# Transposing the gates of a recurrence on two row tiles of TensorE instead of the whole array

## Chip, cores and metric

The kernel runs on one NeuronCore of a Trainium2 chip. The metric is the device time of one execution in microseconds (us); lower is better. The engines are named as in the profile: PE is TensorE (PEld its weight loads), DVE is VectorE, ACT is ScalarE, POOL is GpSimd, SP issues the DMAs.

## What is computed

Two layers stand one after the other, on 4 batches of 6272 time steps and 256 channels, in float32. The first is a gated recurrence over time, the second a long convolution written with Fourier transforms:

```python
sig = 1 / (1 + exp(-f_logit))
f = lower_bound + (1 - lower_bound) * sig
i = 1 - f
for t in range(S):                      # S = 6272
    h = f[:, t] * h + i[:, t] * x[:, t]
    y[:, t] = h
...
proj = y @ w_proj                       # 256 -> 768
x1, x2, x3 = the three thirds of proj
conv = irfft(rfft(x2, axis=1) * rfft(filter, axis=0), n=S, axis=1)
out = (x1 * conv * x3) @ w_out
```

## The kernel before

**An order written by a list scheduler.** The kernel's text does not issue instructions in the order of its loops. Each step is registered with `op(kind, cost, fn, r=, w=, take=, src=)` in a `Plan`: its kind, its assumed cost on each engine that may run it, what it reads and writes, how many of the 8 PSUM banks it takes (`take`), and, for a reader of such banks, the step that filled them (`src`). `Plan.schedule` then places the steps one by one, choosing among those that are ready by the assumed start, with corrections from three tables of constants: `SHY` (by kind and engine), `LEAD` and `TILT` (by kind and batch). `emit` issues the instructions in that order, and each engine runs its own queue strictly in it. A step that takes banks is placed only where a free run of banks is, and only after every other step that its readers need has been placed; its banks come free when the last reader is done. `ROWS` lists the kinds of PE step that work on 64 rows of the array; the plan charges `TURN` (0.097 us) for going from such a step to one on the whole array or back, and prefers, by `STICK`, to stay.

**The recurrence, `hgrn(b)` (L379 to L433).** Time is cut into 13 chunks, 12 of 512 steps (`nb` = 4) and one of 128 (`nb` = 1). For each chunk SP loads `f_logit` into `FL` and `x` into `XT`, with time step `p * nb + j` in partition `p`, block `j` (L389). ACT makes s = sigmoid(-f_logit) in place (`sig`, L392), POOL makes u = x * s in place (`u`, L394). The recurrence runs along time, so s and u must be turned to have channels in partitions and time along the free axis. PE does it in 128x128 float32 transposes (`turn`, L401), one for each block `j`, each half `kh` of the channels and each of s (`sT`) and u (`uT`): with `nb` = 4 four transposes fill one bank of 512 words, each writing every fourth word:

```python
def turn(e, p, src, cols=cols, nb=nb):
    for j in range(nb):
        nc.tensor.transpose(PS[:, p, j:128 * nb:nb], src[:, j, cols], iden[:])
```

The gate f = 1 + nomc * s is made from the bank of s into the float32 tile `fTs`, which has two buffers (`f`, L415 on ACT), and DVE runs the recurrence, reading `fTs` and the bank of u, into the float16 tile `HA` (`scan`, L423). So one chunk and one `kh` have one bank for s and one for u. The first 3072 steps are then copied behind the end (`wrap`).

**The rest of a batch.** `phase_p` (L730) projects `HA` to x2 in groups of 4 time residues, copied out by ACT or DVE (L361, L366). `phase_f1` (L743) and `unit` do the convolution for 16 groups of channels: a forward transform in two steps (L743, and `F2` L788 on 64-row tiles, two matmuls side by side for two adjacent banks), products with the filter's spectrum on DVE (L801), the inverse (L811), copied by ACT (`Th`, L361). `gate` (L450) makes x1 and x3, copied by ACT (L462) and multiplied on POOL (L466). `phase_o` does the last inverse step (L844, 64-row tiles again), a product on DVE (L850), the output projection (L862), a copy on ACT (L363) and the store. All matmuls' results take two adjacent banks but those of `gate`, the warm-up and the transposes, which take one. A preparation ahead of the first batch makes the filter's spectrum (L650, L672, L690, L707, the last two on 64-row tiles). `hgrn(b + 1)` is registered behind `phase_o(b)`, and the schedule lays it beside the convolution and the gate of batch `b`.

Of the kernel before, what the change touches and what calls it, by code (L numbers as in the profile page):

```python
# [13 lines left out]
AOP = mybir.AluOpType  # L14
AF = mybir.ActivationFunctionType
# [42 lines left out]
class Plan:  # L58
# [11 lines left out]
    FROM = {"PE": 0.0, "ACT": 0.0, "DVE": 0.8, "POOL": 0.8, "SP": 0.75}  # L70
    TURN = 0.097
    COLD = 7.5
    SHY = {("A", "ACT"): 27, ("A", "DVE"): 27, ("Th", "ACT"): -10, ("Th", "DVE"): 779,
            ("afs", "ACT"): 51, ("afs", "DVE"): -12, ("f", "ACT"): -4, ("f", "DVE"): 452,
            ("f2", "ACT"): 100, ("f2", "DVE"): 126, ("fr", "ACT"): 290, ("fr", "DVE"): 2705,
            ("fr", "POOL"): -84, ("hw", "ACT"): -32, ("hw", "DVE"): 364, ("o", "ACT"): 13,
            ("o", "DVE"): 1968, ("wrap", "ACT"): 1376, ("wrap", "POOL"): 115, ("x2", "ACT"): 90,
            ("x2", "DVE"): 63}

    STICK = 4.0  # L80
    ROWS = ("F2", "mini", "I1", "FF2", "last")
    LANES = 8

    TILT = {
        "A": (10, -421, 208, -185), "F1": (-87, -1, 1, -163), "F2": (297, -97, -22, -362),
        "FF1": (-72, 0, 0, 0), "FF2": (-79, 0, 0, 0), "H": (-184, 334, 22, 133),
        "I1": (-280, -65, -92, 13), "I2": (-282, -43, -206, 0), "P": (-10, -2, 64, -49),
        "Th": (-3, -372, 21, -100), "afs": (-31, 0, 0, 0), "f": (-348, -382, -7, -601),
        "f2": (206, 0, 0, 0), "ff": (-455, 0, 0, 0), "fr": (-21, 0, 0, 0), "hst": (-91, 0, 0, 0),
        "hw": (11, 0, 0, 0), "load": (-7, -238, -192, 0), "mX": (18, 0, 0, 0),  # L90
        "mini": (-412, 357, -19, 94), "o": (0, -19, 214, 0), "pad": (14, 0, 0, 0),
        "prod": (0, -199, -22, 1135), "proj": (387, -1338, -11, 254), "rot": (-287, 0, 0, 0),
        "sT": (-25, 1516, -37, 149), "scan": (-40, -6, -71, -138), "sig": (-116, 262, -46, -451),
        "slot": (-6, -10, -78, 18), "store": (-23, -498, 174, 242), "tabs": (335, 0, 0, 0),
        "u": (-6, 0, -48, 383), "uT": (-1369, -27, 23, 104), "warm": (-427, 0, 0, 0),
        "wrap": (0, 312, 253, 2), "x13": (-140, -373, -471, -159), "x2": (35, -288, 339, 160),
        "xs": (2160, 1264, 0, 301), "y": (-27, 470, 49, -42), "z": (0, 0, 532, 756),
        "zm": (1130, 0, -12, 65),
    }

    LEAD = {
        "A": (35, -373, 1648, 137), "F1": (462, -629, 1502, 4000), "F2": (5639, 140, 319, 1412),
        "FF2": (-1269, 0, 0, 0), "H": (0, -477, -796, -1751), "I1": (-67, 978, 15, 184),
        "I2": (-35, -8, 4207, 55), "P": (-34, -342, 3292, -57), "Th": (164, 540, 125, 0),
        "args": (598, 0, 0, 0), "f": (294, -69, -69, -264), "f2": (-491, 0, 0, 0),
        "ff": (5684, 0, 0, 0), "fr": (505, 0, 0, 0), "hst": (566, 0, 0, 0), "hw": (-475, 0, 0, 0),
        "iden": (346, 0, 0, 0), "iota": (33, 0, 0, 0), "last": (43, 0, 0, 0),
        "load": (1910, -587, 70, -424), "mX": (103, 0, 0, 0), "mini": (162, -443, 3560, 2034),
        "o": (182, 252, -11, 418), "pad": (-134, 0, 0, 0), "pre": (-656, 0, 0, 0),
        "prod": (53, -700, 0, 7), "proj": (-7749, -9436, -6234, 114), "rest": (109, 0, 0, 0),  # L110
        "sT": (0, -96, -2, -1), "scan": (-892, 17, -1191, -2973), "sig": (0, 79, 43, 146),
        "slot": (126, 219, 502, 1379), "store": (-387, -299, -79, -369), "tabs": (5294, 0, 0, 0),
        "turns": (-46, 0, 0, 0), "u": (801, 3, 107, 648), "uT": (10, -692, -6798, -121),
        "warm": (-40, 0, 0, 0), "wcol": (443, 0, 0, 0), "wl": (-474, 0, 0, 0),
        "wrap": (-936, -549, -39, 333), "x13": (-350, -2412, -46, -1943), "x2": (0, 0, 1048, 2601),
        "xs": (5528, -104, 106, -88), "y": (-100, -570, -30, -285), "z": (-742, -2, 69, 0),
        "zm": (236, 148, 847, -6),
    }

    def __init__(self):  # L120
# [38 lines left out]
    def schedule(self, level):  # L159
# [28 lines left out]
        while base:  # L188
            rooms = {n: self.room(bank, n) for n in (1, 2)}
            best = None  # L190
            for i, b in base.items():
# [8 lines left out]
                for e, a in b.items():  # L200
                    a = max(a, floor, free[e])
                    c = a + (o["cost"][e] * 0.01 if len(b) > 1 else 0.0)
                    c += self.SHY.get((o["kind"], e), 0) / 100
                    stick = self.STICK if e == "PE" and (o["kind"] in self.ROWS) == rows else 0.0
# [73 lines left out]
def kernel(  # L278
# [10 lines left out]
    nc = tc.nc  # L289
# [4 lines left out]
    op = plan.op  # L294

    konst = ctx.enter_context(tc.tile_pool(name="konst", bufs=1))
    iden = konst.tile([128, 128], F32, name="iden")
# [16 lines left out]
    A = HA[:, A0:A0 + AW].rearrange("m (e r k) -> m e r k", r=2, k=64)  # L314
# [16 lines left out]
    FF1 = [("FF1", u, h) for u in range(NU) for h in range(2)]  # L331
    FF2 = [("FF2", u) for u in range(NU)] + ["FF2"]
# [3 lines left out]
    H = [dram.tile([TB + 64, 2 * UE * 64], F16, name=f"H{u}") for u in range(NU)]  # L336
    psp = ctx.enter_context(tc.tile_pool(name="psp", bufs=1, space=PSUM))
    PS = psp.tile([128, 8, 512], F32, name="PS")
# [41 lines left out]
    def hgrn(b):  # L380
        for c in range(NCHK):
            t0 = c * CH
            nb = min(CH, S - t0) // 128
            n = nb * 128
            k = count["x"] % NX
            count["x"] += 1
            xt, ft = XT[:, k, 0:nb], FL[:, k, 0:nb]
            for dst, src, t in ((ft, f_logit, ("ft", k)), (xt, x, ("xt", k))):
                op("load", {"SP": 0.46}, lambda e, dst=dst, src=src, t0=t0, n=n: nc.sync.dma_start(  # L389
                    dst, src[b, t0:t0 + n, :].rearrange("(p j) d -> p j d", p=128)),  # L390
                   w=[t], dma=0.38 * nb, lag=2.4, margin=MARGIN)
            op("sig", {"ACT": 0.095 + 0.213 * nb}, lambda e, ft=ft: nc.scalar.activation(  # L392
                ft, ft, AF.Sigmoid, scale=-1.0), w=[("ft", k)], table="sigmoid")
            op("u", {"POOL": 0.1 + 0.553 * nb}, lambda e, xt=xt, ft=ft: nc.gpsimd.tensor_tensor(  # L394
                xt, xt, ft, op=AOP.mult), r=[("ft", k)], w=[("xt", k)])
            for kh in range(2):
                cols = slice(kh * 128, kh * 128 + 128)

                def turn(e, p, src, cols=cols, nb=nb):
                    for j in range(nb):  # L400
                        nc.tensor.transpose(PS[:, p, j:128 * nb:nb], src[:, j, cols], iden[:])  # L401
                sT = op("sT", {"PE": 0.109 * nb}, lambda e, p, f=turn, s=ft: f(e, p, s),
                        r=[("ft", k), "iden"], w=["qT"], take=1)
                uT = op("uT", {"PE": 0.109 * nb}, lambda e, p, f=turn, s=xt: f(e, p, s),
                        r=[("xt", k), "iden"], w=["qT"], take=1)
                j = count["f"] % 2
                count["f"] += 1
                fT = fTs[:, j, 0:n]
                t1 = HB[kh] + t0
                h = HA[:, t1:t1 + n]  # L410

                def gate_f(e, p, fT=fT, n=n, kh=kh):
                    by = nomc[:, kh:kh + 1]
                    if e == "ACT":
                        nc.scalar.activation(fT, PS[:, p, 0:n], AF.Identity, scale=by, bias=1.0)  # L415
                    else:
                        nc.vector.tensor_scalar(fT, in0=PS[:, p, 0:n], scalar1=by, scalar2=1.0,
                                                op0=AOP.mult, op1=AOP.add)
                op("f", {"ACT": 0.145 + n / 1200.0, "DVE": 0.11 + n / 960.0}, gate_f,
                   r=["om"], w=[("fT", j)], src=sT)  # L420
                init = 0.0 if c == 0 else HA[:, t1 - 1:t1]
                op("scan", {"DVE": 0.12 + 2.08 * n / 1000.0}, lambda e, p, h=h, fT=fT, n=n, init=init:
                   nc.vector.tensor_tensor_scan(h, fT, PS[:, p, 0:n], init, op0=AOP.mult,  # L423
                                                op1=AOP.add),
                   r=[("fT", j)] + ([("hn", kh, c - 1)] if c else []), w=[("hn", kh, c)],
                   src=uT)

                z = min(t0 + n, WR)
                if z <= t0:
                    continue  # L430
                op("wrap", {"POOL": 0.05 + (z - t0) / 1015.0, "ACT": 0.08 + (z - t0) / 1200.0},
                   lambda e, a=t0, z=z, o=HB[kh]: copy(
                       e, HA[:, o + S + a:o + S + z], HA[:, o + a:o + z]),  # L433
                   r=[("hn", kh, c)], w=[("W", kh, i) for i in range(t0 // 1024, (z - 1) // 1024 + 1)])
# [499 lines left out]
```

## Time and profile before

| | |
|---|---|
| median of 3 runs | 507.46 us (506.46 to 508.02) |
| the profiled execution: its own time | 508.43 us |
| the profiled execution: span from first to last instruction | 506.6 us |
| mean granted TensorE clock | 0.988 of full speed |
| busy: PE, DVE, ACT, POOL | 95%, 88%, 81%, 76% of the span |
| DMA: the queue's share of 16 engines, bytes moved | 67.2%, 116.39 MB |
| L401, the transposes | 784 matmuls: 392 of `FL`, 392 of `XT` |
| L415, f on ACT | 104, 69.4 us busy |
| L423, the recurrence on DVE | 104, 96 of them with a start value; 1270 ns for one such of 512 steps |

Busy time of PE is read with care: the end of a matmul is modelled and holds its way through the array, so matmuls that follow each other overlap in the records, and the time that one really costs is the distance from start to start.

### The profile page before, as it was taken

To read this page: it belongs to the slowest core of one execution; us is meant where nothing else is said; L and a number is where in the kernel's file an instruction comes from. 1 tells how busy PE (TensorE), PEld (TensorE's weight loads), DVE (VectorE), ACT (ScalarE), POOL (GpSimd) and SP (SyncE) were. 2 spreads that over 40 slices of the span, in tenths; PEclk is the share of its full clock that TensorE was granted. 3 is DMA by queue.
4 is the path that set the end of the run, shared out by engine and by line. 5 is a ranking of instruction groups with operands and counts; after the bars stand their busy time and mean duration, and the time that the engine had idled before them with its cause. 6 is when DMAs were issued, how large, how long until landed. Compare 5 with 4: busy or idle time off the path is not lost.

```text
span 506.6 us, 13245 instructions
## 1 busy us (share of the span) xinstructions
PE 481.4 (95%) x5257; PEld 375.4 (74%) x5257; DVE 443.9 (88%) x451; ACT 411.1 (81%) x587; POOL 386.5 (76%) x328
## 2 busy tenths in 40 slices
PE   8979997999999999999999999999999999999795
PEld 6767775867767899866767899667778997666584
DVE  8789987789899999898997999989999988988663
ACT  3658867889999877898899787899989867999554
POOL 8886766789999864499899858789998733998700
PEclk9999999899999999999999999999999999999889
DMA  8979998716668999246678898156788960345056
GB/s 334 408 224 298 305 295 292 220 35 219 213 200 272 286 339 372 99 134 195 180 233 279 290 344 346 31 177 187 246 296 301 340 258 12 101 134 155 29 237 273
DMA packets 41725, 116.39 MB, mean 230 GB/s; under 512 B 4384, under 2 KB 6304, under 8 KB 41664
## 3 DMA queue, kind: packets, MB, share of 16 engines
q1 hardware_dynamic: 41664, 115.56, 67.2%
q8 instruction: 41, 0.67, 0.6%
q14 instruction: 20, 0.16, 0.1%
HBM read 84.54 MB, written 31.00 MB: 228 GB/s over the span
## 4 chain that ended last, share of the span: by engine, by line
PE 63%; DVE 10%; DMA 8%; issue 6%; ACT 6%; POOL 5%; SPq 0%; POOLq 0%; ACTq 0%; DVEq 0%
PE PS L450 11%; PE PS L401 10%; PE PS L862 9%; PE PS L730 8%; PE PS L811 5%; DMA H<-Hu 5%; PE PS L743 5%; PE PS L788 4%; PE PS L844 4%; POOL zt L466 4%; PE PS L621 3%; DVE PP L801 3%; DVE HA L423 2%; DMA FL<-in_f_logit_dram 2%; DVE X L366 2%
## 5 line engine op out<-in xcount | busy, mean ns | idle before, releaser
L466 POOL TENSOR_TENSOR zt<-x1s,x3s 128x490 f16<-128x490 f32 (+1 forms) x104 | 201.6, 1952 | 42.5 <-ACT x3s L462 26.1
L801 DVE TENSOR_TENSOR PP<-PS,Hu 98x1008 f16<-98x1008 f32 x128 | 146.8, 1199 | 11.2 <-ACT x1s L462 3.7
L394 POOL TENSOR_TENSOR XT<-XT,FL 128x1024 f32<-128x1024 f32 (+1 forms) x52 | 117.2, 2257 | 33.6 <-DMA XT<-in_x_dram 13.6
L423 DVE TENSOR_TENSOR_SCAN HA<-fTs,HA,PS 128x512 f16<-128x512 f32 (+1 forms) x96 | 114.1, 1204 | 11.8 <-PE PS L401 7.8
L450 PE MATMUL PS<-HA,W 128*128 128x490 f16 (+1 forms) x416 | 107.7, 371 | 1.5 <-DVE PP L801 1.0
L415 ACT ACTIVATE fTs<-PS,nomc 128x512 f32<-128x512 f32 (+1 forms) x104 | 69.4, 669 | 18.8 <-PE PS L401 13.2
L850 DVE TENSOR_TENSOR ys<-PS,zt 128x1024 fp32r<-128x1024 f32 (+1 forms) x52 | 59.9, 1158 | 13.7 <-PE PS L844 6.6
L363 ACT ACTIVATE osb<-PS 128x1024 f32<-128x1024 f32 (+1 forms) x52 | 50.5, 978 | 21.6 <-PE PS L862 20.9
L462 ACT ACTIVATE x1s<-PS 128x490 f32<-128x490 f32 (+1 forms) x104 | 60.8, 585 | 5.7 <-PE PS L450 3.8
L401 PE MATMUL PS<-iden,XT 128*128 128x128 f32 x392 | 62.6, 280 | 2.1 <-POOL XT L394 1.1
L462 ACT ACTIVATE x3s<-PS 128x490 f32<-128x490 f32 (+1 forms) x104 | 60.6, 584 | 3.9 <-POOL zt L466 1.7
L862 PE MATMUL PS<-Wo,ys 128*128 128x256 f32 x392 | 60.8, 298 | 2.1 <-DVE ys L850 1.2
L401 PE MATMUL PS<-iden,FL 128*128 128x128 f32 x392 | 60.6, 275 | 1.1 <-ACT Hu L363 0.8
L811 PEld LDWEIGHTS <-PP 98*128 98x128 f16 x1024 | 50.1, 98 | 10.7 <-issue 2.4
L392 ACT ACTIVATE FL<-FL 128x1024 f32<-128x1024 f32 (+1 forms) x52 | 52.4, 1011 | 5.4 <-DMA FL<-in_f_logit_dram 5.4
L361 ACT CAST Th<-PS 128x784 f16<-128x784 f32 x64 | 52.8, 824 | 4.5 <-PE PS L811 4.0
L862 PEld LDWEIGHTS PS<-Wo,ys 128*128 128x128 f32 x392 | 51.1, 194 | 6.1 <-DVE ys L850 1.9
L450 PEld LDWEIGHTS <-W 128*128 128x128 f16 x416 | 35.0, 98 | 27.5 <-issue 9.7
L401 PEld LDWEIGHTS PS<-iden,XT 128*128 128x128 f32 x392 | 44.2, 141 | 14.5 <-POOL XT L394 2.8
L811 PE MATMUL PS<-VA,PP 98*128 98x98 f16 x512 | 52.4, 207 | 1.5 <-DVE PP L801 0.7
L811 PE MATMUL PS<-VB,PP 98*128 98x98 f16 x512 | 52.1, 207 | 0.0
L366 DVE CAST X<-PS 128x1024 f16<-128x1024 f32 (+1 forms) x34 | 47.0, 1487 | 5.2 <-PE PS L730 3.9
(98 smaller groups left out, 702.0 us busy)
## 6 DMA issues: line engine op xcount, KB each, us to landing
Hu<-H SPq DMA_DIRECT2D x64, 392.0 KB
FL<-in_f_logit_dram SPq DMA_DIRECT2D x48, 512.0 KB
XT<-in_x_dram SPq DMA_DIRECT2D x48, 512.0 KB
out_dram<-osb SPq DMA_DIRECT2D x48, 512.0 KB
X<-in_moe_filter_fft_dram SPq DMA_DIRECT2D x9, 512.0 KB
H<-Hu SPq DMA_DIRECT2D x16, 196.0 KB
H<-Hu SPq DMA_DIRECT2D x16, 128.0 KB
Hu<-in_moe_filter_fft_dram SPq DMA_DIRECT2D x2, 512.0 KB
```

The source lines that it names most:

```text
L366: nc.vector.tensor_copy(dst, src)
L394: op("u", {"POOL": 0.1 + 0.553 * nb}, lambda e, xt=xt, ft=ft: nc.gpsimd.tensor_tensor(xt, xt, ft, op=AOP.mult), r=[("ft", k)], w=[("xt", k)])
L401: nc.tensor.transpose(PS[:, p, j:128 * nb:nb], src[:, j, cols], iden[:])
L415: nc.scalar.activation(fT, PS[:, p, 0:n], AF.Identity, scale=by, bias=1.0)
L423: nc.vector.tensor_tensor_scan(h, fT, PS[:, p, 0:n], init, op0=AOP.mult, op1=AOP.add),
L450: nc.tensor.matmul(PS[:, p, 0:n], W13[:, kh, js], HA[:, HB[kh] + t0:HB[kh] + t0 + n], start=(kh == 0), stop=(kh == 1))
L462: nc.scalar.activation(xs(i), PS[:, p, 0:n], AF.Copy, scale=1.0 if i else ZS),
L466: nc.gpsimd.tensor_tensor(late["zt"][:, jb, :, m0:m0 + nm], xs(0).rearrange("p (m r) -> p r m", r=Q), xs(1).rearrange("p (m r) -> p r m", ...
L801: nc.vector.tensor_tensor(PP[:TB, k, o, :, :, 1:64], px.unsqueeze(1).broadcast_to([TB, 2, UE, 63]), hh[:, :, :, 1:64], op=AOP.mult)
L811: nc.tensor.matmul(PS[:, ib + o, pr * TB:(pr + 1) * TB], PP[:TB, k, o, n, 2 * pr:2 * pr + 2, :], v[:TB], start=(n == 0), stop=(n == 1))
L850: nc.vector.tensor_tensor(late["ys"][:, yk, :, 0:rn * 128], PS[:, cb:cb + 2, 0:rn * 128], late["zt"][:].rearrange("p k r m -> p k (r m)") ...
L862: nc.tensor.matmul(po[:, i, :], late["ys"][:, yk, kh, i * 128:(i + 1) * 128], Wo[:, kh, :], start=(kh == 0), stop=(kh == 1))
```

## The change

s and u are no longer transposed in 128x128 blocks. Each block of 128 time rows is split into its upper and its lower 64 rows (`a` = 0, 1), which lie on two row tiles of the array, and each becomes a matmul in transpose mode with 64 rows, 128 weight columns (the data) and 64 moving columns (a 64x64 part of the identity). The outputs of the two row tiles go to two adjacent banks. Both halves `kh` of the channels are turned in one step, whose two banks hold them word by word in turn: the time step t of half `kh` is word 2t + kh of the run. For `nb` = 4 that fills both banks; the run is placed around the border of the two (from word 512 - n), so that one stepped run reads one half through both. So `sT` and `uT` are one step for each chunk instead of one for each `kh`, of 16 matmuls instead of 4, and take two banks instead of one. Each write steps by 2 * nb words instead of nb; `f` and `scan` read every second word. `sT` and `uT` join `ROWS`, their assumed cost changes, and the constants of `SHY`, `TILT` and `LEAD` are other ones, so the order on every engine changes.

```diff
-    SHY = {("A", "ACT"): 27, ("A", "DVE"): 27, ("Th", "ACT"): -10, ("Th", "DVE"): 779,
+    SHY = {("A", "ACT"): 11, ("A", "DVE"): 25, ("Th", "ACT"): -11, ("Th", "DVE"): 358,
...
-    ROWS = ("F2", "mini", "I1", "FF2", "last")
+    ROWS = ("F2", "mini", "I1", "sT", "uT", "FF2", "last")
...
+            def run(p, at, m, step):
+                return PS[:, p:p + 2].rearrange("m a n -> m (a n)")[:, at:at + (m - 1) * step + 1:step]
+            def turn(e, p, src, nb=nb, n=n, run=run):
+                for j in range(nb):
+                    for kh in range(2):
+                        for a in range(2):
+                            rows = slice(64 * a, 64 * a + 64)
+                            nc.tensor.matmul(run(p, 512 - n + a * n + kh + 2 * j, 64, 2 * nb),
+                                             src[rows, j, kh * 128:kh * 128 + 128], iden[rows, rows],
+                                             is_transpose=True, start=True, stop=True)
+            sT = op("sT", {"PE": 0.145 * nb}, lambda e, p, f=turn, s=ft: f(e, p, s),
+                    r=[("ft", k), "iden"], w=["qT"], take=2)
+            uT = op("uT", {"PE": 0.145 * nb}, lambda e, p, f=turn, s=xt: f(e, p, s),
+                    r=[("xt", k), "iden"], w=["qT"], take=2)
             for kh in range(2):
-                cols = slice(kh * 128, kh * 128 + 128)
-                def turn(e, p, src, cols=cols, nb=nb):
-                    for j in range(nb):
-                        nc.tensor.transpose(PS[:, p, j:128 * nb:nb], src[:, j, cols], iden[:])
-                sT = op("sT", {"PE": 0.109 * nb}, lambda e, p, f=turn, s=ft: f(e, p, s),
-                        r=[("ft", k), "iden"], w=["qT"], take=1)
-                uT = op("uT", {"PE": 0.109 * nb}, lambda e, p, f=turn, s=xt: f(e, p, s),
-                        r=[("xt", k), "iden"], w=["qT"], take=1)
...
-                        nc.scalar.activation(fT, PS[:, p, 0:n], AF.Identity, scale=by, bias=1.0)
+                        nc.scalar.activation(fT, run(p, at, n, 2), AF.Identity, scale=by, bias=1.0)
...
-                   nc.vector.tensor_tensor_scan(h, fT, PS[:, p, 0:n], init, op0=AOP.mult,
+                   nc.vector.tensor_tensor_scan(h, fT, run(p, at, n, 2), init, op0=AOP.mult,
```

Here `at` is 512 - n + kh. How the new tables move the work is read from the two programs' orders. PE goes between 64-row and whole-array matmuls 326 times instead of 280. The transposes stand in 86 unbroken groups instead of 112, and 42 of those groups follow a whole-array matmul. ACT and DVE hold the same steps with a few of them exchanged: of the 64 copies behind L743, DVE has 12 instead of 18; of the 48 full copies behind L730 it has 31 instead of 30; of the 32 copies behind L672 28 instead of 32; of the copies behind L650 (24 full ones and 2 of a quarter) it has 8 full and the 2 small ones instead of 11 full; ACT has the others. All 104 `f` stay on ACT, all 104 `scan` on DVE. POOL and SP hold the same steps in another order, DMAs included.

## Prediction, made before the changed kernel was run

> **What bounds the kernel now.** I read the page's busy times first, then its slices, then the chain that ended last, then the busy times by stage. The first three lines here are from the page: PE's row of busy times, and the slices of PE and DVE (tenths of a fortieth of the span, 12.7 us each). The fourth is the chain's shares by line.
>
> ```profile
> PE 481.4 (95%) x5257; PEld 375.4 (74%) x5257; DVE 443.9 (88%) x451; ACT 411.1 (81%) x587; POOL 386.5 (76%) x328
> PE   8979997999999999999999999999999999999795
> DVE  8789987789899999898997999989999988988663
> by line: PE PS L450 10.9%; PE PS L401 10.5%; PE PS L862 9.2%; PE PS L730 7.9%; issue 6.3%; PE PS L811 5.4%; DMA H<-Hu 5.0%; PE PS L743 4.8%; PE PS L788 4.5%; PE PS L844 4.3%; POOL zt L466 3.7%; PE PS L621 2.8%; DVE PP L801 2.6%; DVE HA L423
> ```
>
> PE is full and holds most of the chain; L401, the line that changes, is its second largest item with 10.5% of 506.6 us, 53.2 us. But DVE is near as full. By stage (start:end, then length and busy time of PE, PEld, DVE, ACT, POOL; the last row is the whole stretch in which transposes run, L401 starting from 30.4 to 410.3 us):
>
> ```profile
> 115.00:215.00 100.00, 98.31 (x1179) 79.10 (x1178) 93.85 (x88) 87.47 (x123) 78.21 (x62) 1.00 0.74 251
> 215.00:315.00 100.00, 96.75 (x1128) 76.52 (x1127) 92.59 (x87) 86.32 (x129) 87.30 (x67) 1.00 0.76 253
> 315.00:410.00 95.00, 94.40 (x1132) 73.57 (x1130) 89.10 (x83) 84.59 (x128) 79.90 (x63) 1.00 0.67 225
> 30.00:410.00 380.00, 367.35 (x4019) 287.92 (x4017) 347.50 (x329) 324.81 (x468) 307.01 (x244) 1.00 0.73 242
> ```
>
> The reader is to see that PE comes first (95 to 99%), DVE second (93 to 94%) and ACT third (86 to 89%). Time taken from PE is worth something until DVE and ACT run out of slack. Outside 30 to 410 us there is no transpose, so nothing to win.
>
> **What a transpose costs, and a row-tile pair.** The timeline, whose columns are start, length, engine, line and count (matmuls' ends hold their way through the array, so I take distances of starts):
>
> ```profile
> 30.45 0.42 PEld L401 LDWEIGHTS PS<-iden,FL 128*128 128x128 f32 x4 [0.39 <-issue]
> 32.34 0.60 PE L401 MATMUL PS<-iden,FL 128*128 128x128 f32 x4
> 83.70 0.42 PEld L707 LDWEIGHTS PS<-mX,FTr 64*98 64x98 f32 x8 [0.55 <-POOL mX L681]
> 106.98 0.58 PE L450 MATMUL PS<-HA,W 128*128 128x490 f16 x2
> 107.49 0.61 PE L788 MATMUL PS<-HA,FT 64*128 64x256 f16 x8
> 108.03 0.59 PE L450 MATMUL PS<-HA,W 128*128 128x490 f16 x2
> 109.52 0.61 PE L743 MATMUL PS<-D,X 128*128 128x128 f16 x8
> ```
>
> - Four transposes in a stream: (0.60 - 0.273 of one) / 3 = 0.109 us each, 784 of them 85.5 us. L743 with as many columns in float16 takes (0.61 - 0.219) / 7 = 0.056. So a float32 transpose moves a column in 0.85 ns.
> - The loads hide under that. In the first row, a burst after idle, the four loads span 0.42 - 0.14 = 0.28; two steps of 0.109 leave 0.06 for the first, which is a load alone.
> - Row tiles do run side by side: L788 has eight matmuls of 256 columns in (0.61 - 0.27) / 3 = 0.113 a pair, where one of 256 on the whole array (L730) takes 0.109. L707 shows it in float32: (0.42 - 0.16) / 3 = 0.086 a pair, with 98 weight columns and 128 moving ones.
> - A turn between 64 rows and the whole array costs 0.095: L450's second matmul starts at 107.19, L788 at 107.49, 0.30 later, where a matmul of 490 columns takes 0.206.
>
> A new pair has 128 weight columns and 64 moving ones. No row shows it. From below: its moving part is 64 x 0.85 = 0.055, its load 0.057. From above: 0.109, if the two tiles take turns or the wider step of the writes costs as much as the halved columns save. The nearest row is L707's 0.086, whose float32 weights load more slowly. I take the middle between 0.057 and 0.086, 0.072.
>
> **The sum on PE.** 784 pairs replace 784 transposes: 784 x (0.109 - 0.072) = 29.0 us saved. 46 turns more (326 for 280): 4.4 us lost. 42 groups of transposes now follow a whole-array matmul, and their first load can't hide across the turn: 42 x 0.057 = 2.4 us lost. Net 22.2 us, between 34.0 (pair at 0.057) and -6.8 (at 0.109).
>
> **What of it reaches the end.** Of 85.5 us of transposes 53.2 lie on the chain, 0.62. I take the net saving at that share: 22.2 x 0.62 = 13.8 us. The rest lies where a load, DVE or POOL was late anyway.
>
> **What the readers must bear.** The new order takes work off DVE: six copies of L743 (1.217 each), four of L672 (0.678) and three less two small ones of L650 (about 1.3 in all), against one more of L730 (1.508): 7.3 + 2.7 + 1.3 - 1.5 = 9.8 us. ACT gets about 6.1 + 2.8 + 1.5 - 1.5 = 8.9. In a stretch of 380 - 13.8 = 366 us DVE is then (347.5 - 9.8) / 366 = 92% busy, as now, ACT (324.8 + 8.9) / 366 = 91%, two points above its fullest stage. So the forecast asks something of ACT.
>
> **Edits that I cost at nothing.** `f` and `scan` read every second word, over two banks. ACT reads such steps at full rate in `Th` (L361: 784 words, 98 apart, in 824 ns; copies of 256 and 1024 words in a row take 413 and 1025, so 834 for 784). The scan takes 1.270 us for 512 words, more than twice as long a word as a copy of words in a row (1.217 for 1024), so it has time to step. If the step cost what it may cost in L730's copies, which also write in short runs (1494 for 1025 on ACT, 1508 for 1217 on DVE, for 1024 words), it would be 0.23 us in each `f` and 0.15 in each `scan`, 24 and 15 us in all; from the other side nothing is gained. I take nothing, by the nearer row, `Th`. SP issues the same DMAs in another order; their share of 0.73 leaves room.
>
> **Two rules that speak against it.** Of the writes: the Trainium skill, "PSUM — Partial Sum Buffer", Specifications, says that PSUM has lines of 8 bytes and that outputs that aren't contiguous slow matmuls much. The transposes of before already write every fourth word, and whether that or float32 makes their 0.85 ns a column no row here shows. If the cost grew with the step, a pair would be at 0.109 and the sum at the slower rival below; if it comes with leaving the line, nothing changes. Of the readers: "TensorEngine Tiling (Array Packing)", PSUM Bottleneck, says that tiling speeds up TensorE but not the emptying of PSUM. The rows of DVE and ACT above bear it out, and by it the sum would be nearer to the first rival.
>
> **Rivals**, from 508.4 us, the profiled execution's own time (1.0 above the median of the runs, 507.46; what I give is put on the median's scale by taking off 1.0):
>
> - Forecast: 508.4 - 13.8 = 494.6, given as 493.6. Own range 487 to 500.
> - The readers become the bound. ACT stays at the 89% of its fullest stage: (324.8 + 8.9) / 0.89 = 375 us for the stretch, 5 saved, 502.4. For it: ACT's copies stand between PE and POOL, and POOL already waits longest for them (26.1 us on L462). Against: the chain holds 63% PE and 6% ACT.
> - More is saved: pair at 0.057, 34.0 x 0.62 = 21.1, 486.4; nearly all of 34.0 if the new order keeps DVE full, 474. For it: DVE is given 9.8 us less.
> - The pair saves nothing (0.109): 6.8 x 0.62 = 4.2 lost, 511.6. Then the change doesn't do what it says. For it: no transpose on row tiles in the trace. Against: L707 and L690 load float32 in pairs.
> - Slower through PSUM. Two whole pairs of banks of the four are held per chunk, one until both `f`, one until both `scan` are done; before, single banks came back after one reader. If PE, strictly in order, waits for one `f` (0.694) in each of 52 chunks, that is 36.1 us against 22.2 saved, and 13.9 x 0.62 = 8.6 lost, 516. It decides from 22.2 / 52 = 0.43 us of waiting a chunk. For it: all else but the gate's matmuls needs pairs too. Against: PE's idle time before L401 now comes to some 3 us.
>
> **How the numbers follow.** Chances: forecast 0.55; readers 0.18; more saved 0.10; pair saves nothing 0.05; PSUM 0.12. Within 0.3% (1.5 us, about what a measurement of this kernel can tell from no change) I put 0.05, where the readers' case and the PSUM case meet and their costs cancel, 0.03 from the first and 0.02 from the second: faster 0.80, same 0.05, slower 0.15. The range goes from 483, halfway into the case that saves more, to 510, and leaves out some 0.06 below and 0.13 above.
>
> **What would show it.** The new transposes' starts: 16 in about 0.072 x 8 = 0.58 us, tiles of a pair some 3 ns apart. PE's busy share falls below 93% with DVE's at 88 to 91% or more. `f` at about 694 ns and `scan` at 1270 say that reading every second word is free. Idle time of PE ended by L415 or L423 above 22 us would be the PSUM rival. I am wrong if the pairs stand 0.1 apart, or if ACT's and DVE's rows grow.

## The result, and the profile after

The changed kernel takes 521.4 us (median of 4 runs, 519.22 to 524.25) against 507.16 of the kernel before: a ratio of 1.0283, interval 1.0225 to 1.0342. It is 2.8% slower, where 2.7% faster was forecast. The profiled execution takes 524.25 us, its span is 522.5. Some executions of a program run slower as a whole, at a lower granted clock; ratios leave them out (four of run 17's six, at most one of any other run).

The page of the changed kernel: busy times, the slices of PE, DVE and of the clock granted to PE, and the chain's shares by engine.

```profile
PE 468.0 (90%) x6041; PEld 353.5 (68%) x6041; DVE 431.8 (83%) x441; ACT 416.8 (80%) x597; POOL 385.5 (74%) x328
PE   7997868989998888989998997999998999999796
DVE  8778866897998885989898996988798988988764
PEclk9999998999999998999997998999999999999889
PE 51%; DVE 12%; ACT 12%; DMA 11%; POOL 7%; issue 6%; SPq 0%; ACTq 0%; DVEq 0%; POOLq 0%
```

PE's busy share fell from 95 to 90%, as forecast, but nothing else filled up: DVE went from 88 to 83%, about half of that because it has 12 us less to do, half because the span grew. All engines wait more. PE's share of the chain fell from 63 to 51%; DVE (12 for 10), ACT (12 for 6), DMA (11 for 8) and POOL (7 for 5) have the rest.

The edit itself does what it says. A step of 16 transposes in the changed kernel's timeline (matmuls and their loads), and the steps that read the banks, by form (the last two lines are those of the kernel before; behind the second bar stands the engine's idle time before them and what ended it):

```profile
168.73 0.69 PE L405 MATMUL PS<-iden,FL 64*128 64x64 f32 x16
168.68 0.61 PEld L405 LDWEIGHTS PS<-iden,FL 64*128 64x128 f32 x16
...
L431 DVE TENSOR_TENSOR_SCAN HA<-fTs,HA,PS 128x512 f16<-128x512 f32 x88 | 108.6, 1267 | 22.0 <-PE PS L405 15.9 <-ACT fTs L423 4.8 <-ACT x1s L470 1.2
L423 ACT ACTIVATE fTs<-PS,nomc 128x512 f32<-128x512 f32 x96 | 61.2, 689 | 17.0 <-PE PS L405 15.4 <-DVE ys L858 0.8 <-DVE HA L431 0.4
L423 DVE TENSOR_TENSOR_SCAN HA<-fTs,HA,PS 128x512 f16<-128x512 f32 x88 | 110.6, 1270 | 7.2 <-PE PS L401 5.0 <-ACT fTs L415 1.8
L415 ACT ACTIVATE fTs<-PS,nomc 128x512 f32<-128x512 f32 x96 | 66.5, 694 | 17.8 <-PE PS L401 12.1 <-DVE nomc L496 2.7 <-DVE HA L423 1.9
```

Eight pairs take (0.69 - 0.22) / 7 = 0.067 us each, the exposed first load among it (in the middle of a group pairs start 0.063 apart, by the median), where a whole-array transpose takes 0.109. Reading every second word costs nothing: 1267 ns for the scan (1270 before), 689 for f (694). But both readers now wait longer for the transposes, DVE 15.9 us where it was 5.0, and ACT 15.4 where it was 12.1.

So where did the time come from? The first projection to x2 (L730, now L738) of a batch needs all of that batch's recurrence, so it marks the batches. Where it starts for the second batch, before and after:

```profile
196.57 0.33 PE L730 MATMUL PS<-W,HA 128*128 128x256 f16 x1
```

```profile
207.21 0.43 PE L738 MATMUL PS<-W,HA 128*128 128x256 f16 x1
```

The marks lie at 91, 197, 307, 413 and the end at 507 us before; at 92, 207, 321, 428 and 522 after. The preparation costs the same; the stretch up to the second mark loses 10 us, the one up to the third 4, the one up to the fourth nothing, and 1 to 2 go after the last mark. I call these the second, third and fourth batch. In the stage in which the output of the first batch meets the recurrence of the second, all is less busy (start:end, length, busy PE, PEld, DVE, ACT, POOL, clock, DMA share, GB/s; the kernel before, then the changed one):

```profile
165.00:195.00 30.00, 29.72 (x379) 25.68 (x377) 29.28 (x26) 24.24 (x33) 20.04 (x20) 1.00 0.95 323
```

```profile
165.00:207.00 42.00, 34.35 (x532) 27.60 (x530) 31.58 (x29) 32.32 (x47) 24.91 (x18) 0.99 0.95 323
```

PE was busy 99% of this stage, DVE 98%. Now it is 82 and 75%, the mark that ends the stage comes 10.6 us later, and only DMA is as busy. The order shows one difference there: before, the last three groups of the first batch's output come behind the mark (their projection, L862, starts at 207, 209 and 234 us); after, all 13 groups come ahead of it, by 197 us, beside the loads and transposes that the mark waits for.

### The profile page after: what moved, and what is told of

Same layout as the page of the kernel before. It is cut to its first block, busy times and chain, and to the rows that moved or that the text cites. A ratio compares the mean times of both kernels' runs of the same rounds, so it can differ in the third digit from the quotient of the medians.

```text
span 522.5 us, 14805 instructions
## 1 busy us (share of the span) xinstructions
PE 468.0 (90%) x6041; PEld 353.5 (68%) x6041; DVE 431.8 (83%) x441; ACT 416.8 (80%) x597; POOL 385.5 (74%) x328
## 4 chain that ended last, share of the span: by engine, by line
PE 51%; DVE 12%; ACT 12%; DMA 11%; POOL 7%; issue 6%; SPq 0%; ACTq 0%; DVEq 0%; POOLq 0%
PE PS L458 10%; PE PS L738 7%; PE PS L870 7%; PE PS L405 6%; PE PS L819 6%; DVE PP L809 5%; PE PS L796 4%; DMA FL<-in_f_logit_dram 4%; PE PS L751 4%; DMA H<-Hu 4%; DMA out_dram<-osb 3%; PE PS L852 3%; DVE HA L431 3%; ACT osb L363 3%; DVE X L366 2%
## 5 line engine op out<-in xcount | busy, mean ns | idle before, releaser
L431 DVE TENSOR_TENSOR_SCAN HA<-fTs,HA,PS 128x512 f16<-128x512 f32 (+1 forms) x96 | 112.0, 1200 | 27.1 <-PE PS L405 17.7
L423 ACT ACTIVATE fTs<-PS,nomc 128x512 f32<-128x512 f32 (+1 forms) x104 | 63.9, 664 | 17.8 <-PE PS L405 15.8
L858 DVE TENSOR_TENSOR ys<-PS,zt 128x1024 fp32r<-128x1024 f32 (+1 forms) x52 | 58.8, 1152 | 16.5 <-PE PS L852 12.8
L870 PE MATMUL PS<-Wo,ys 128*128 128x256 f32 x392 | 59.4, 296 | 2.7 <-DVE ys L858 1.3
L819 PE MATMUL PS<-VA,PP 98*128 98x98 f16 x512 | 53.8, 209 | 5.7 <-DVE PP L809 2.5
L361 ACT CAST HA<-PS 128x1024 f16<-128x1024 f32 x52 | 52.7, 1026 | 5.0 <-PE PS L751 4.7
L366 DVE CAST X<-PS 128x1024 f16<-128x1024 f32 (+1 forms) x35 | 48.8, 1479 | 9.3 <-PE PS L738 9.2
L819 PE MATMUL PS<-VB,PP 98*128 98x98 f16 x512 | 53.6, 209 | 0.0
L738 PE MATMUL PS<-W,HA 128*128 128x256 f16 x392 | 45.4, 278 | 0.8 <-DVE X L366 0.5
L405 PE MATMUL PS<-iden,FL 64*128 64x64 f32 x784 | 37.8, 235 | 8.3 <-ACT X L363 3.7
```

What stands on the lines that cost most here:

```text
L361: nc.scalar.copy(dst, src)
L405: nc.tensor.matmul(run(p, 512 - n + a * n + kh + 2 * j, 64, 2 * nb), src[rows, j, kh * 128:kh * 128 + 128], iden[rows, rows], is_transpose ...
L431: nc.vector.tensor_tensor_scan(h, fT, run(p, at, n, 2), init, op0=AOP.mult, op1=AOP.add),
L738: nc.tensor.matmul(pp[:, r - r0, :], column(HB[kh], q_of(r)), W2[:, kh, :], start=(kh == 0), stop=(kh == 1))
L819: nc.tensor.matmul(PS[:, ib + o, pr * TB:(pr + 1) * TB], PP[:TB, k, o, n, 2 * pr:2 * pr + 2, :], v[:TB], start=(n == 0), stop=(n == 1))
L870: nc.tensor.matmul(po[:, i, :], late["ys"][:, yk, kh, i * 128:(i + 1) * 128], Wo[:, kh, :], start=(kh == 0), stop=(kh == 1))
```

## The experiments

Ratios are to the kernel before, run on the same chip; its medians lay between 504.8 and 507.9 us.

**1. The changed order with whole-array transposes.** Every instruction of every other engine stays in the changed kernel's order; only the transposes and the two readings go back, with one bank for each half.

```diff
-                for j in range(nb):
-                    for kh in range(2):
-                        for a in range(2):
...
+                for kh in range(2):
+                    for j in range(nb):
+                        nc.tensor.transpose(PS[:, p + kh, j:128 * nb:nb],
+                                            src[:, j, kh * 128:kh * 128 + 128], iden[:])
```

> The changed kernel with every instruction of every engine in the changed kernel's order, but the transposes whole-array again: both halves of the channels in one step of 8, each half in a bank of its own, words in a row for the readers. The changed kernel profiles at 524.3 us, its pairs start some 0.06 us apart, so 784 transposes at 0.109 put about 38 us back on PE and take a part of the 326 turns away. Theory A (the order is to blame, the row tiles pay): slower than the changed kernel, 528 to 545 us. Theory B (two banks held per step are to blame): the banks are held as long, so slower too, 525 to 545. Theory C (the row tiles themselves, their turns, their clock or the stepped reading cost the time): faster than the changed kernel, 505 to 515.

Measured: 524.89 us, ratio 1.0384 (1.0326 to 1.0442). The row tiles are no loss: without them the time is 1.0% longer, some 5 us. But they take 784 x (0.109 - 0.067) = 32.9 us from PE and put 64 turns (326 for 262 in this program), 6.1 us, back: net 27 us, and 5 of these are seen. The other finding is larger: with whole-array transposes as before and nearly the same work on every engine (ACT is busy 6 us more, DVE 11 us less), this program is 3.8% slower. Its busy times and the clock granted to PE:

```profile
PE 483.6 (93%) x5257; PEld 377.4 (73%) x5257; DVE 433.1 (83%) x441; ACT 417.0 (80%) x597; POOL 385.1 (74%) x328
PEclk9999999999999999999999999999999999999889
```

Theory C fell. Theories A and B had expected 528 and 525 us or more; this run can't tell them apart, since the order and the banks held in pairs are both in it.

**2. Half of the transposes left out of the kernel before.**

```diff
+                    m = (nb + 1) // 2
-                    for j in range(nb):
-                        nc.tensor.transpose(PS[:, p, j:128 * nb:nb], src[:, j, cols], iden[:])
+                    for j in range(m):
+                        nc.tensor.transpose(PS[:, p, j:128 * m:m], src[:, j, cols], iden[:])
```

> The kernel before, its order and its banks untouched, with only the first two of the four blocks of a full chunk transposed, so that the recurrence's input is not the right one: f reads the 256 words twice, the scan reads one word again and again, both as many words as before. 384 transposes of 0.109 us, 42 us of PE, are gone and nothing else. If time taken from PE's transposes is worth 0.62 of itself as the prediction had it: 26 us, 481 us. If DVE and ACT bound the kernel already: 495 us or more. If the order is so tight that only PE counts: below 475.

Measured: 501.31 us, ratio 0.9899 (0.9862 to 0.9936). 42 us less on PE, in the order of before, with its banks and without a turn more, give 5 us: 0.12 of it, not 0.62 (the clock granted to PE is lower too, 0.984 by the median of the runs for 0.991). PE's busy time in this kernel, on its page:

```profile
PE 454.2 (90%) x4873; PEld 336.1 (67%) x4873; DVE 441.5 (88%) x451; ACT 409.7 (82%) x587; POOL 384.9 (77%) x328
```

It fell by 27 us in the records (481.4 before), which overlap matmuls, and the other engines' shares stayed at 88, 82 and 77%.

**3 and 4. Half of the stores left out**, in the changed kernel and in the one before (`r0:r0 + (rn + 1) // 2` for `r0:r0 + rn`; half of the output is not written).

> The changed kernel storing only half of the rows of each group of outputs: the rest of the output is left unwritten, 13 MB less for the DMA queue. Theory A in its sharper form (the new order puts all stores of the first batch beside the loads of the second, and DMA is the bound from 165 to 207 us): 8 us faster or more, 505 to 514. If the stores have nothing to do with it: 518 to 522.

> The kernel before storing half of the rows of each group, the control for the same edit of the changed kernel. Theory A: the order of before spreads the stores, so 1 to 4 us faster at most, 503 to 506. If DMA binds both kernels alike: 8 us faster or more, below 499.

Measured: 516.33 us, ratio 1.0214 (1.0159 to 1.0268), and 505.32 us, ratio 0.9972 (0.9931 to 1.0012). The changed kernel gains 0.7%, between the two ranges expected, against 0.3% that are within noise. In the second batch, where I looked for it, nothing comes back: its marks lie at 89.7 and 204.8 us, 115.1 apart for 115.5, though DMA's share from 165 to 207 us fell from 0.95 to 0.81. So DMA is not what makes that stage longer, and the sharper form of theory A fell. What this one execution gains lies ahead of the first mark (2 us) and in the third batch (109 us for 114).

**5 and 6. DVE relieved, alone and with PE.** A plain product takes the recurrence's place in the kernel before (`tensor_tensor` for `tensor_tensor_scan`).

> The kernel before, its order, banks and transposes untouched, with a plain product of the gate and u in place of the recurrence (so the recurrence is left out and the output is another one): 96 instructions on DVE of some 0.65 us instead of 1.27, about 58 us of DVE gone. Theory DVE (taking 42 us from PE was worth only 5 because DVE takes PE's place at once): DVE's time is worth much, 485 us or less. Theory D (in a fixed order the five queues hold each other so tightly that no one engine's time is worth much): 497 to 504 us. If PE is still the only bound: no change, 505 to 508.

> Both cuts at once: half of the transposes left out as in the run with half of them, and the plain product in place of the recurrence; the output is another one. 42 us of PE and 58 us of DVE gone, order untouched. Theory DVE: now the saving on PE shows, 470 us or less. Theory D: about the sum of the two single gains, and still far from the 42 us, 485 to 498, since ACT, POOL and DMA remain with their places in the queues.

Measured: 505.52 us, ratio 0.9979 (0.9943 to 1.0015), and with half of the transposes left out as well 500.32 us, ratio 0.9852 (0.9799 to 0.9905). DVE's busy time in the first of the two:

```profile
PE 480.1 (95%) x5257; PEld 375.4 (74%) x5257; DVE 391.7 (78%) x451; ACT 409.8 (81%) x587; POOL 386.0 (77%) x328
```

52 us less on DVE (443.9 before) are worth nothing that can be told from noise, and both cuts together 7 us. Theory DVE fell. Theory D, that the queues hold each other, had expected somewhat more of each run (497 to 504 and 485 to 498 us). The first lies where PE as the only bound had put it, but run 2 speaks against that. What still stands in the way can be read by stage. First the kernel before, beside the convolution and beside the output, then the run with both cuts in the same stretches:

```profile
115.00:165.00 50.00, 49.21 (x604) 35.96 (x603) 47.26 (x46) 47.71 (x75) 48.22 (x39) 1.00 0.69 226
165.00:195.00 30.00, 29.72 (x379) 25.68 (x377) 29.28 (x26) 24.24 (x33) 20.04 (x20) 1.00 0.95 323
```

```profile
115.00:165.00 50.00, 47.50 (x575) 31.88 (x572) 42.98 (x48) 48.15 (x77) 48.83 (x38) 1.00 0.68 226
165.00:195.00 30.00, 26.02 (x328) 22.45 (x327) 22.65 (x26) 23.65 (x31) 18.70 (x19) 1.00 0.99 343
```

The kernel before alternates between two stages. Beside the convolution PE is busy 98%, DVE 95%, ACT 95% and POOL 96%; beside the output PE 99%, DVE 98% and DMA 0.95. With PE and DVE relieved, ACT and POOL stand at 96 and 98% in the first, and DMA at 0.99 in the second.

**7 and 8. Constants found anew for both kernels.** SHY, LEAD and TILT start from zeros and are changed at random for a fixed time, with the time that the plan itself computes for its schedule (its own account) as the measure; nothing else is changed.

> The changed kernel's steps, banks and row tiles, but its constants SHY, LEAD and TILT found anew: started from zeros, by a random search of fixed length over the plan's own account. To be compared with the next kernel alone, which had the same search. Theory A (only the constants of the changed kernel are poor, its steps are as good or better): equal to the next kernel within 4 us, or faster. Theory B (steps of two banks for both halves cost, whatever the order): 10 us or more slower than the next kernel. Both are expected above the changed kernel's 521 us, 525 to 545, since the search is short.

> The kernel before with its constants SHY, LEAD and TILT found anew in the same way, from zeros, with the same length of search. The counterpart of the run ahead of it: under theory A this one is as slow or slower, under theory B it is 10 us or more faster. 525 to 545 us; that it is far slower than the kernel before, with the same steps, would show how much of a time lies in the constants.

Measured: 534.65 us, ratio 1.053 (1.0469 to 1.0592), and 536.95 us, ratio 1.0552 (1.0491 to 1.0613). With equally poor constants the two sets of steps are equal; the old steps lose 29 us by their constants alone. That speaks against theory B, but less than it seems: run 13 below takes the row tiles out of run 7 again and is 1.7% slower than run 8. So the equality is a gain of some 9 us by row tiles and a loss of some 8 by the rest, be it the banks held in pairs or an order planned for cheaper transposes.

**9 and 10. Banks of u without a reader.** The scan reads the gate's buffer in place of the bank of u, in the order of run 1 and in the kernel before.

```diff
-  nc.vector.tensor_tensor_scan(h, fT, PS[:, p + kh, 0:n], init, op0=AOP.mult, op1=AOP.add)
+  nc.vector.tensor_tensor_scan(h, fT, fT, init, op0=AOP.mult, op1=AOP.max)
```

> The kernel of the first run (changed order, whole-array transposes in two banks), with the scan reading the gate's buffer in place of the bank of u, with max in place of the sum: u is left out of the recurrence, the output is another one. Every instruction stays in its place, but the two banks of uT have no reader and come free with the transposes' end, and the scan no longer waits for them. Theory B (banks held in pairs for two scans starve the other steps): 10 us or more below the first run's 524.9. Theory F (the order of the steps itself, with its loop of inverse, product, projection, copy and the bank pair that goes around in it, sets the pace): within 4 us of 524.9.

> The kernel before with the same edit, u left out of the recurrence, the output another one: the control. Theory B: 0 to 4 us faster than before, since single banks come back soon anyway. Theory F: the same.

Measured: 608.67 us, ratio 1.2055 (1.1967 to 1.2143), and 593.0 us, ratio 1.1711 (1.1612 to 1.1809). Inconclusive, since the scan now waits for POOL. Its row in the ninth run's groups, for 512 steps, and two pairs of scans in its timeline with what POOL does beside the first (beside the second POOL is idle):

```profile
L428 DVE TENSOR_TENSOR_SCAN HA<-fTs,HA 128x512 f16<-128x512 f32 x88 | 188.1, 2170 | 6.6 <-ACT fTs L420 6.5
184.76 10.82 DVE L428 TENSOR_TENSOR_SCAN HA<-fTs,HA 128x512 f16<-128x512 f32 x2
184.45 2.36 POOL L394 TENSOR_TENSOR XT<-XT,FL 128x1024 f32<-128x1024 f32 x1
186.75 3.17 POOL L471 TENSOR_TENSOR zt<-x1s,x3s 128x392 f16<-128x392 f32 x2
189.85 2.38 POOL L394 TENSOR_TENSOR XT<-XT,FL 128x1024 f32<-128x1024 f32 x1
192.13 1.20 POOL L371 COPY HA<-HA 128x512 f16<-128x512 f16 x2
499.62 2.44 DVE L428 TENSOR_TENSOR_SCAN HA<-fTs,HA 128x512 f16<-128x512 f32 x2
```

A mean of 2170 ns for 1267 in run 1 buries whatever the banks are worth.

**11 and 12. Everything else relieved.** In the kernel before: the plain product (DVE 52 us less), u = x * s left out (POOL), the copies of x1 left out and x3 squared (ACT), half of each store left out (DMA); then half of the transposes left out too.

> The kernel before, its order and its full transposes untouched, and all other resources relieved: a plain product for the recurrence (DVE some 52 us less), u = x * s left out (POOL 117 us less), the copies of x1 left out and x3 squared instead (ACT some 60 us less), half of each store left out (DMA 12.5 MB less). Theory G (in each stage of a batch several resources are full at once, ACT and POOL at 96% beside the convolution, DMA at 95% beside the output, so that what is taken from PE alone is not seen): PE is now the only one that is full, 490 to 503 us. Theory D (the queues' waits for each other, whatever is full): 500 us or more.

> The same with half of the transposes left out too, 42 us less on PE. Theory G: PE's time is now worth what the prediction took it to be worth, 20 us or more below the run ahead of it. Theory D: 5 to 8 us below it, as with half of the transposes alone.

Measured: 499.2 us, ratio 0.9874 (0.9793 to 0.9955), and 485.58 us, ratio 0.9589 (0.9506 to 0.9671). The difference, 13.6 us for 42 on PE, is two and a half times what the same cut gave alone, so the other resources hide a part of PE's time (theory G). But it is a third, not the 20 us or more expected, even with ACT at 75%, DVE at 80% and POOL at 37%. I take it that the queues, whose order was written for other durations, wait for each other (theory D); that was not tested by itself. The page of the last one:

```profile
PE 450.0 (92%) x4873; PEld 339.3 (70%) x4873; DVE 388.5 (80%) x451; ACT 365.5 (75%) x483; POOL 180.6 (37%) x276
PEclk9998997999999999999998999999979999999889
```

**13, 14 and 15. Other constants for the changed steps.** Run 14 has constants from a longer search that started near the changed kernel's own; runs 13 and 15 are runs 7 and 14 with whole-array transposes, as in run 1.

> The kernel with constants found anew for the changed steps (534.65 us), in its order, with whole-array transposes in the two banks. How much of the 38 us that row tiles take from PE is seen in another order than the changed kernel's. If about a tenth, as in the changed kernel's order (3.5 us): 537 to 540. If a looser order gives PE's time its full worth: 550 or more. If row tiles cost something: 534 or less.

> The changed kernel with better constants: a longer search over the plan's own account, started near the changed kernel's. Steps, banks and row tiles as in the changed kernel. Theory A (the changed kernel is slow by the order that its constants give): 506 to 514, most of the 14 us back with the same steps. Theory B (two banks held per step cost whatever the order): 518 or more.

> The run ahead of this one, in its order, with whole-array transposes in the two banks. If a tenth of PE's saving is seen: 3 to 5 us slower than the run ahead. If that order lets PE be the bound: 12 us or more slower.

Measured: run 13, 543.27 us, ratio 1.0717 (1.0683 to 1.0751); run 14, 511.33 us, ratio 1.01 (1.0063 to 1.0137); run 15, 517.25 us, ratio 1.0217 (1.0191 to 1.0243). Run 14 is the changed kernel but for its constants, and 10 of its 14 us are back. Its page:

```profile
PE 459.0 (90%) x6041; PEld 347.3 (68%) x6041; DVE 433.8 (85%) x445; ACT 415.4 (82%) x593; POOL 385.5 (76%) x328
PEclk9999999999999999999999999999999999999999
```

PE is as little busy as in the changed kernel (90%), the time is 1.8% shorter, and the clock hardly drops (0.990 by the median of the runs, where the changed kernel has 0.976). Against it run 15 says what row tiles are worth in this order, 1.2% or 6 us; run 13 against run 7 says 1.9% or 9 us. In three orders, then, 5 to 9 of some 27 us. Run 13 lies between the two ranges expected of it, run 15 just above the lower one.

**16, 17 and 18. Banks once more, and chance.** Run 16 is run 1 with the plain product of run 5, which gives uT's banks back 0.6 us earlier for each scan; 17 and 18 are the changed kernel with two more sets of constants of nearly the same account as run 14.

> The first run's kernel (changed order, whole-array transposes in two banks) with a plain product in place of the recurrence, which is left out: DVE has some 52 us less, and the two banks of uT come free 1.2 us earlier in each chunk. Theory B (the banks held for two scans are what costs the changed order): 10 us or more below the first run's 524.9, where the same edit of the kernel before gave 2. Theory A (the order alone): 2 to 6 us below it.

> The changed kernel with a second set of better constants from the same kind of search, of nearly the same account as the first set (511.33 us). Theory A: 506 to 516, and the differences between the sets say how much of a time is the order's chance. Below 505 it would beat the kernel before.

> The changed kernel with a third set of better constants, again of nearly the same account: 506 to 516, and below 505 it would beat the kernel before.

Measured: run 16, 521.08 us, ratio 1.0271 (1.0227 to 1.0315), 1.1% below run 1, where the same edit gave the kernel before 0.2%: within what theory A expected and short of theory B's 10 us. Run 17, ratio 1.0145 (1.0074 to 1.0216), with runs from 511.83 to 521.37 us; run 18, 511.61 us, ratio 1.0086 (1.0049 to 1.0122). No order tried with the new steps beats the kernel before, and orders that the plan holds for nearly equal differ by 0.6% (runs 14, 17 and 18), which their intervals don't tell apart.

## Why the prediction was wrong

Two steps failed. Of the 28 us between the forecast (13.8 us less) and the result (14.2 us more) the first has 8.7, the second, a term put at nothing, 19.5.

- **"What of it reaches the end" failed.** I took the net saving at the chain's share of L401, 0.62, and had 13.8 us; the row tiles are worth 5.1 in the changed order (run 1). Measured, PE's time is worth 0.12 of itself in the order of before (run 2), some 0.2 to 0.35 for the row tiles themselves (runs 1, 13 to 15), and 0.32 with the other resources relieved (runs 11 and 12). A share of one chain says what was waited for last, not what would be waited for next. That other engines were late by little beside PE's work is what runs 11 and 12 suggest; they relieve several at once, and two thirds of the time cut from PE stay hidden even so.
- **"What bounds the kernel now" read the wrong windows.** I took stretches of 100 us, saw ACT at 86 to 89% and POOL at 78 to 87%, and concluded that there was slack. Each stretch mixes two stages: in the first ACT and POOL are at 95 and 96%, in the second DMA is at 0.95. With windows of one stage the rows above would have said that there is little behind PE to win.
- **The new order had no term in the sum, and it turned the sign.** I counted which copies change engines and took the order for neutral, without a reason. With whole-array transposes it costs 3.8%, 19.5 us (run 1), more than all that I priced; the banks held in pairs are in that number. Other constants for the same steps take 1.8% of the loss back (run 14). The first step alone would have made the forecast too good, not wrong in direction.
- **What a pair costs** was mis-sized on the safe side: 0.067 with its first load, where the sum had 0.072 plus 2.4 us for loads. The 326 turns are as counted. On PE the forecast was 22.2 us, the measured pair gives 32.9 - 4.4 = 28.5.
- **Reading every second word at nothing** was right, 1267 for 1270 ns and 689 for 694. The writes' wider step cost nothing that shows either: 64 columns in at most 0.063 us, by which the rule on PSUM's lines had its milder reading.
- **The rivals.** The PSUM rival, 516 us, had the right side, but not by the wait that it named: of PE's idle time before L405 (matmuls and loads counted together) f and scan ended 2.9 and 5.9 us, where it needed 22. That its number comes near is luck. The first of the changed kernel's rows:

```profile
its engine sat idle before it (us, times) until:
  issue: 9.0, 17
  ACT osb L363: 8.3, 8
  ACT X L363: 7.6, 2
  DVE HA L431: 5.9, 12
  ACT HA L361: 3.1, 5
  ACT fTs L423: 2.9, 6
```

  ACT's copies of other steps end more of it, 8.3 and 7.6 us. Whether those are waits for their banks, that is, whether pairs of banks cost a few us in this order, stays open: it could not be taken apart from the order. That the readers become the bound was right in part (run 12) and too weak, since it spoke of ACT alone and of averages.
- **Of my signs** the clearest was DVE's share, 88 to 91% or more in the forecast. It is 83%: an engine that was to fill up emptied, and run 1, with all of PE's work back, has 83% too. That points at the order, not at PE.

Shown, then: the row tiles work and are worth 5 to 9 us in the orders tried; the loss is in the order of the new steps, and 10 of its 14 us go with other constants. What costs the 10 us of the second batch was not settled. Where the second mark lies is telling: at 197 us in the two programs that do all the work with the old steps (before and run 8), at 202 to 219 in all ten with steps of two banks, run 14 among them (202; run 9, whose scan waits for POOL, is left aside). In those ten all of the first batch's output stands ahead of that mark or within 1 us of it, but the two go together, and neither was tried without the other; the stores alone are not it (run 3). So the last 1% may lie in the banks held in pairs, in that place of the output, or in constants not found.

## What to carry to other kernels

Before a saving on the fullest engine is priced, cut the profile into windows of one stage and list every resource above 90% in each; if there are three, expect far less than the chain's share of the saving (here a tenth to a third, not 0.62). In a kernel whose queues are laid out by a scheduler, a changed cost changes the whole order, and the order is a term of its own, here as large as all the rest: undo the edit in the new order to see the two apart. Halving an engine's work, with the result thrown away, is a cheap test of what its time is worth.

## What the runs showed of the hardware that I had not expected

- A scan that reads both operands from SBUF waits for POOL. In run 9 it takes a mean of 2170 ns for 512 steps, where one with an operand from PSUM takes 1267 (run 1). Beside an idle POOL it is as fast as ever: the pair at 499.62 us takes 2.44 us, and the 21 with hardly any of POOL's work beside them have a median of 1259 ns. So neither max in place of the sum nor the second operand from SBUF costs anything by itself. The pair at 184.76 us takes 10.82: POOL's instructions run without a break until 193.3, and the first of the two scans ends 1.1 us later. POOL's own small steps grow too (the 512-word copy of L371 from 625 ns in run 1 to 847, the cast of L686 from 204 to 842). The Trainium skill, "SBUF — State Buffer", Who interferes with whom, says that a DVE instruction with two inputs in SBUF and a GpSimd instruction that reads SBUF contend for a shared pair of ports, and that this pair is an exclusive lock; the rows agree with that.
- A PE with less to do was granted less clock, in all six pairs of programs that differ in little but PE's transposes. By the median of the runs: 0.976 of full speed with row tiles and 0.991 with whole-array transposes in the changed order (run 1), 0.977 and 0.980 (runs 7 and 13), 0.990 and 0.993 (14 and 15); with half of the transposes and with all 0.984 and 0.991 (run 2 and before), 0.977 and 0.991 (6 and 5), 0.989 and 0.996 (12 and 11). PE's busy share alone doesn't fix it, since the changed kernel and run 14 both have 90%. So a part of what is taken from PE can return as slower matmuls, by estimate up to 0.015 x 521 = 8 us in the changed kernel. It isn't the main loss: run 1 has the clock of before and is the slower one.
- Row tiles take float32 transposes at 0.063 us a pair, 64 columns and 128 weight columns, mostly some 3 ns between the two, each going into its own bank with a step of eight words.
